# One matmul stage by a rank-20 block algorithm in place of 22 block products, with new sums of its inputs

## The chip, the cores and the metric

One core of one Trainium2 chip runs the whole program in one launch. The metric is the device time of the launch in microseconds (us); three runs of the kernel before took 589.03, 589.66 and 590.48 us (median 589.66).

## The reference

`r`, `k`, `v`, `w` have batch 4, 8 heads, 768 steps and 48 features a head; everything is float32.

```
state = 0
for t in range(768):
    cur  = (u*k[t]) outer v[t]
    y[t] = r[t] @ (state + cur)
    state = w[t][:, None]*state + k[t] outer v[t]
x   = y as 3072 tokens x 384 features
h   = x @ w_in            # 384 x 2048
g   = 0.5*h*(1 + erf(h/sqrt(2)))
out = g @ w_out           # 2048 x 384
```

The change concerns `h = x @ w_in` and, through its results, the sums of `g` that feed the last product.

## The kernel before, in words

The 3072 tokens are eight tiles of 384 tokens (`T`). For tile x there is `attention(x)`, which leaves the tile's y transposed in `xT` (3 blocks of 128 features by 384 tokens), and `mlp(x)`, which makes h, GELU and the output. Both are Python generators that yield after each small piece. While `mlp(x-1)` runs, the main loop also runs most of `attention(x)` and the first steps of `attention(x+1)`: a string `PLAN[x]` has one letter for each piece to be issued next ("." is `mlp`, "s" the attention slots of this tile, "f" the following tile's, "x" the sums of xT, "w" masks and sums of weights, "l" loads, "c" conversion of weights). There is no scheduler: each engine works off its own queue in exactly the order in which the letters issue. The queues are TensorE (PE), VectorE (DVE), ScalarE (ACT), GpSimd (POOL, here only the issuing of DMAs that add to memory) and SyncE (SP, loads and stores).

**h in mlp(1) to mlp(7)** (`h_halves`, matmuls at L929). The tokens are cut in halves of 192, the features in three blocks of 128, and w_in's columns in two halves; 22 block products replace 24 by means of sums of blocks. It goes in four rounds (q), each for two blocks of 128 columns from each half. One `two(...)` with one pair of factors is two matmuls of 128x128 by 128x192. Seven sub-steps a round leave their results in three PSUM banks; ACT copies a bank to another bank (L972) or to g (L995, L999) or to a buffer `o_sb` (L965), and a finished block goes through GELU (L961, L958). What is saved in `o_sb` is added to g by a DMA that accumulates, issued by POOL (L980), in the first three rounds, and by DVE (L982) in the last. The sums of xT are five DVE instructions (`sums_of_x`, L897); the sums of w_in are made once by DVE (`h_sums`, L880 to L888), between mlp(0) and mlp(1).

**The output** is a second set of block products (L1073) over g, over sums of g (`of_g`, L921 to L925, DVE) and over sums of w_out. Its first product reads blocks of g for the first 128 tokens, its second those of the second 128 tokens, its third needs an ACT copy of the first (`p1`, L1109).

**Attention beside it.** In tiles 2 to 7 (`quarters`) DVE multiplies and reduces r, k and w (L378, L385, L411, L419), ACT and DVE lay out `kx` (L557, L562, L563), PE then makes scores into a pair of banks `d` (L588, L579), which DVE and ACT copy out (L621, L604). DVE updates r and k (L642, L649, L653), and after a second round of the same PE makes kv and y (L711, L752, L797). At the end of a tile ACT copies y to xT (L820, L823), SP moves 16 rows of it (L827), and DVE makes the sums of xT for the next mlp.

PSUM holds two banks `mm` (h and o), two banks `u` and two pairs `d`. A bank can be written again only when its last reader is done. mlp(0) makes h without sums (L1059).

Of the kernel before, what the change touches and what calls it, by code (L numbers as in the profile page):

```python
# [10 lines left out]
F32 = mybir.dt.float32  # L11
# [31 lines left out]
        "ccclfccccccfccfcccccfccfccwf.ff......fw.sl.w.x.wx...x..x...xww"  # L43
    ),
    2: (
        "s.s.....ss....ssw.ws.wl.wsss.wws.s..lsl...lws.w..s.ww....s.s..l..sss.lssss....s..s..s.sls."
        "llsf.sf.fs..fl.xx.x.fxx"
    ),
    3: (
        "ls.ls....lss..ss.....ss..l.s.lsss.sss.s.s.s.ss..sss..sssssss....s.s..l...s..l.sslslsf.ffs."  # L50
        "..x.lx..xxx"
    ),
    4: (
        "lls.s.sss..s.l.........ssss.....sss.s.ss.s..s.sllss...s.s..l.sss.ss..s.ss...s..sslsll.s..f"
        ".sf.sf..ff..xx.xflxx"
    ),
    5: (
        "..ss...s..ssl....sls...s.sss..sss..sss.sls...sllss..sssss.s..l..s.s...s.slll..s.ssfsf.fsf."
        "....xxx.lxx"
    ),  # L60
    6: (
        "ss..sss...s.....s.sl..s...l.s.ssls.s.s..s..sssssl......ss.ssss.sl.sl...s.....ss..llsssl.f."
        "s.fsf.f.f.xx.l.xffxx"
    ),
    7: "....ss.s...s.s.s....s.sss..ss.ss.sss..s..sss..sssssss......s.s....s..ssss.s...x.x..xxx",
}

# [6 lines left out]
def kernel(  # L74
# [276 lines left out]
    xT_of = {}  # L351

    def attention(x, unit):
# [14 lines left out]
        if x not in xT_of:  # L368
            xT_of[x] = wk.tile([128, NJ, T], F32, name="xT")
        xT = xT_of[x]  # L370
# [483 lines left out]
    HK = HF // 2  # L854
    s_of, x_sums, s12_of = [], [], {}

    def homes():

        more = [cv.tile([128, PIECE], I64, name="s", tag="raw", bufs=AHEAD).bitcast(F32) for _ in range(2)]
        s3_sb.append(more[0][:, 0:HF * 128].rearrange("p (f c) -> p f c", f=HF))  # L860
        x_sums.extend(z[:, i * HT:(i + 1) * HT] for z in (more[0][:, HF * 128:], more[1][:, HF * 128:]) for i in range(2))
        spare = [cv.tile([128, PIECE], F32, name=name) for name in ("f", "f", "e", "e")]
        for i, name in enumerate(("s1", "s2")):
            s12_of[name] = [z[:, 0:FG * 128].rearrange("p (f c) -> p f c", f=FG) for z in spare[2 * i:2 * i + 2]]
        second = [more[1][:, i * WI:(i + 1) * WI] for i in range(HK)]
        third = [s_home[:, i * WI:(i + 1) * WI] for i in range(HK)]
        fourth = [z[:, FG * 128:] for z in spare]
        s_of.extend((second, third, fourth))

    def h_sums():  # L870

        def w(a, c, k):
            return w_in_sb[:, a * HK + k * 2:a * HK + k * 2 + 2, c, :]

        def pieces_of(i, k):
            return s_of[i - 2][2 * k:2 * k + 2]

        for k in range(2):
            for i in range(2):
                nc.vector.tensor_sub(pieces_of(3, k)[i], w(0, 0, k)[:, i], w(1, 0, k)[:, i])  # L880
            yield
            nc.vector.tensor_add(w(1, 0, k), w(1, 0, k), w(1, 1, k))
            yield
            for i in range(2):
                nc.vector.tensor_sub(pieces_of(2, k)[i], w(1, 0, k)[:, i], w(0, 0, k)[:, i])
            yield
            for i in range(2):
                nc.vector.tensor_sub(pieces_of(4, k)[i], w(0, 1, k)[:, i], pieces_of(2, k)[i])  # L888
            yield

    def sums_of_x(x):

        xT = xT_of[x]
        x00, x01, x10, x11, l0, l1 = (xT[:, c, b * HT:(b + 1) * HT] for c in range(3) for b in range(2))
        t2, t3, t4, l01 = x_sums
        for o, a, b in ((t3, x11, x01), (x01, x01, x00), (t2, x11, x01), (t4, x10, t2), (l01, l0, l1)):
            nc.vector.tensor_sub(o, a, b)  # L897
            yield

    def mlp(x):  # L900
# [3 lines left out]
        xT = xT_of.pop(x)  # L904
# [26 lines left out]
        late = []  # L931

        def h_halves():

            x00, t1, x10, x11, l0, l1 = (xT[:, c, b * HT:(b + 1) * HT] for c in range(3) for b in range(2))
            t2, t3, t4, l01 = x_sums

            def w(a, c):
                return lambda f: w_in_sb[:, (a * HF + f) // FI, c, f % FI * 128:(f % FI + 1) * 128]

            def s(i):
                return w(1, 0) if i == 1 else lambda f: s_of[i - 2][f // FI][:, f % FI * 128:(f % FI + 1) * 128]

            def two(o, q, *factors, start=False):
                for i in range(2):
                    for n, (lhs, rhs) in enumerate(factors):
                        multiply(o[:, i * HT:(i + 1) * HT], lhs(2 * q + i), rhs, start and i == n == 0)

            def of_two(o):
                return o.rearrange("p (f t) -> p f t", f=2)  # L950

            def g_of(q, a, b):
                return gs[2 * a + 2 * q // FG][:, 2 * q % FG:2 * q % FG + 2, b * HT:(b + 1) * HT]

            def gelu(q, a, b, z):
                o = g_of(q, a, b)
                if waits and b:
                    nc.scalar.activation(out=o[:, :, 0:256 - HT], in_=z[:, :, 0:256 - HT], func=AF.Gelu)  # L958
                    f = a * HF + 2 * q
                    o, z = alone[:, f:f + 2], z[:, :, 256 - HT:]  # L960
                nc.scalar.activation(out=o, in_=z, func=AF.Gelu)  # L961

            def saved(o):
                z = wk.tile([128, DM], F32, name="o_sb", bufs=2)
                nc.scalar.copy(out=z, in_=o)  # L965
                return of_two(z)

            def first(q):
                a_of[q] = h_bank()
                two(a_of[q], q, (w(0, 0), x00), start=True)  # L970
                u_of[q] = bank_u(q)[:, 0:2 * HT]
                nc.scalar.copy(out=u_of[q], in_=a_of[q])  # L972

            def second(q):
                two(a_of[q], q, (w(0, 1), x10), (w(0, 2), l0))
                gelu(q, 0, 0, of_two(a_of[q]))

            def add_to(q, z, g):
                if q < HK - 1:
                    nc.gpsimd.dma_start(out=g, in_=z, accum_op=ALU.add)  # L980
                else:
                    nc.vector.tensor_add(g, g, z)  # L982

            def third(q):
                two(z_of[q], q, (s(4), x11), (w(0, 2), l1))
                add_to(q, saved(z_of[q]), g_of(q, 0, 1))

            def fourth(q):
                two(u_of[q], q, (w(1, 1), t4), (w(1, 2), l01))
                gelu(q, 1, 0, of_two(u_of[q]))  # L990

            def fifth(q):
                z_of[q] = h_bank()
                two(z_of[q], q, (s(1), t1), start=True)
                nc.scalar.copy(out=g_of(q, 1, 1), in_=of_two(z_of[q]))  # L995

            def sixth(q):
                two(u_of[q], q, (s(2), t2))
                nc.scalar.copy(out=g_of(q, 0, 1), in_=of_two(u_of[q]))  # L999

            def seventh(q):
                two(u_of[q], q, (s(3), t3), (w(1, 2), l1))
                add_to(q, saved(u_of[q]), g_of(q, 1, 1))

            def h_bank():
                return bank("h_ps")[:, 0:2 * HT]

            a_of, z_of, u_of = {}, {}, {}
            for group in (0, 2, 1, 3):
                gs[group] = gp.tile([128, FG, T], F32, name="g")  # L1010
            for q in range(HK):
                first(q)
                yield
                if q:
                    third(q - 1)
                    if q > 1:
                        gelu(q - 2, 1, 1, g_of(q - 2, 1, 1))
                    yield
                    seventh(q - 1)
                    yield  # L1020
                else:
                    fifth(q)
                    yield
                second(q)
                yield
                if q:
                    fifth(q)
                    yield
                sixth(q)
                yield  # L1030
                if q:
                    fourth(q - 1)
                    gelu(q - 1, 0, 1, g_of(q - 1, 0, 1))
                    yield
            q = HK - 1
            seventh(q)
            gelu(q - 1, 1, 1, g_of(q - 1, 1, 1))
            yield
            third(q)
            for _ in of_g(0):  # L1040
                pass
            yield

            def rest():
                fourth(q)
                gelu(q, 0, 1, g_of(q, 0, 1))
                gelu(q, 1, 1, g_of(q, 1, 1))
# [270 lines left out]
```

## Time and profile before

| | |
|---|---|
| runs | 589.03, 589.66, 590.48 us |
| span of the profiled execution | 587.8 us (the page gives it no other time: the median run lies 1.9 us above) |
| granted TensorE clock, mean | 0.997 |
| DMAs that add to g (POOL) | 42 of 192 KB |
| MLP's first matmuls of h start at | 118.8, 190.8, 254.3, 325.7, 389.3, 460.6, 524.5 us |

Busy time by stretch, us:

| stretch | length | PE | DVE | ACT | POOL |
|---|---|---|---|---|---|
| 0 to 44 | 44.0 | 32.2 | 34.2 | 17.4 | 8.0 |
| 44 to 115, with mlp(0) | 71.0 | 71.0 | 61.6 | 57.5 | 0.0 |
| 115 to 187, mlp(1) | 72.0 | 72.0 | 58.4 | 33.8 | 7.3 |
| 187 to 254, mlp(2) | 67.0 | 66.3 | 50.3 | 32.5 | 7.2 |
| 254 to 322, mlp(3) | 68.0 | 68.0 | 55.4 | 33.0 | 7.2 |
| 322 to 389, mlp(4) | 67.0 | 66.7 | 51.2 | 32.7 | 7.2 |
| 389 to 460.6, mlp(5) | 71.6 | 71.1 | 57.7 | 33.5 | 7.2 |
| 460.6 to 524.5, mlp(6) | 63.9 | 63.6 | 41.0 | 32.4 | 7.2 |
| 524.5 to 555, mlp(7), h | 30.5 | 30.5 | 3.9 | 15.5 | 7.2 |
| 555 to 588, mlp(7), output | 33.0 | 29.8 | 11.7 | 3.2 | 0.0 |

In a timeline each row is: start, length (both us from the span's start), engine, line, operation, output and input, shape, count, and in brackets how long the engine had been idle and what ended that. One matmul in the program is two MATMUL records in the trace (float32 goes in two passes). Rows of the chain of waits are start, length, engine, output, line and number of pieces.

### The profile page before, as it was taken

To read this page: it belongs to the slowest core of one execution; us is meant where nothing else is said; L and a number is where in the kernel's file an instruction comes from. 1 tells how busy PE (TensorE), PEld (TensorE's weight loads), DVE (VectorE), ACT (ScalarE), POOL (GpSimd) and SP (SyncE) were. 2 spreads that over 40 slices of the span, in tenths; PEclk is the share of its full clock that TensorE was granted. 3 is DMA by queue.
4 is the path that set the end of the run, shared out by engine and by line. 5 is a ranking of instruction groups with operands and counts; after the bars stand their busy time and mean duration, and the time that the engine had idled before them with its cause. 6 is when DMAs were issued, how large, how long until landed. Compare 5 with 4: busy or idle time off the path is not lost. (4 is left out here: it accounts for less than half of the span.)

```text
span 587.8 us, 17656 instructions
## 1 busy us (share of the span) xinstructions
PE 571.1 (97%) x7602; PEld 521.4 (89%) x7616; DVE 425.5 (72%) x825; ACT 291.2 (50%) x668; POOL 58.6 (10%) x63
## 2 busy tenths in 40 slices
PE   5789999999999999999999999999999999999997
PEld 3576666799999999999999999999998999999997
DVE  5988968989758975777959986777759987420332
ACT  2368898446362567235462467245561467335400
POOL 3100000013000130012000130002100111003100
PEclk8999999999999999999999999999999999999999
DMA  6749742253032542354122632344224333114201
GB/s 230 221 135 352 265 168 78 79 142 52 5 89 64 157 58 41 90 142 93 26 55 79 151 70 44 86 139 74 27 41 119 86 42 42 29 45 55 28 13 35
DMA packets 62430, 55.09 MB, mean 94 GB/s; under 512 B 32400, under 2 KB 47504, under 8 KB 62352
## 3 DMA queue, kind: packets, MB, share of 16 engines
q1 hardware_dynamic: 50832, 45.62, 25.5%
q0 software_dynamic: 11424, 8.26, 10.8%
q8 instruction: 60, 0.98, 0.7%
q14 instruction: 18, 0.15, 0.1%
q10 hardware_dynamic: 96, 0.07, 0.1%
HBM read 36.24 MB, written 4.72 MB: 70 GB/s over the span
## 5 line engine op out<-in xcount | busy, mean ns | idle before, releaser
L929 PE MATMUL h_ps<-xT,w_in_sb 128*128 128x192 f32 x560 | 111.5, 330 | 0.6 <-DVE o_sb L1196 0.6
L980 POOL DMA_DIRECT2D g<-o_sb x42 | 50.6, 1229 | 478.2 <-ACT o_sb L965 468.9
L929 PEld LDWEIGHTS h_ps<-xT,w_in_sb 128*128 128x128 f32 x560 | 93.0, 190 | 4.7 <-ACT g L961 1.6
L929 PE MATMUL u_ps<-s,w_in_sb 128*128 128x192 f32 x224 | 41.2, 327 | 0.0
L1073 PE MATMUL o_ps<-w_out_sb,g 128*128 128x192 f32 x224 | 39.8, 326 | 0.0
L929 PEld LDWEIGHTS u_ps<-s,w_in_sb 128*128 128x128 f32 x224 | 37.1, 190 | 0.2
L1073 PEld LDWEIGHTS o_ps<-w_out_sb,g 128*128 128x128 f32 x224 | 37.0, 190 | 0.0
L604 ACT COPY a_sb<-d 32x256 f32<-32x256 f32 (+8 forms) x90 | 32.6, 362 | 4.9 <-PE d L588 3.4
L1059 PE MATMUL h_ps<-xT,w_in_sb 128*128 128x384 f32 x96 | 33.2, 494 | 0.0
L452 PEld LDWEIGHTS d<-rkw 64*64 64x64 f32 x1152 | 19.4, 138 | 14.7 <-issue 10.5
L1073 PE MATMUL o_ps<-w_out_sb,f 128*128 128x192 f32 x176 | 32.0, 331 | 0.0
L1073 PE MATMUL o_ps<-t,g 128*128 128x192 f32 x176 | 31.4, 330 | 0.0
L1073 PE MATMUL o_ps<-t,s 128*128 128x192 f32 x176 | 31.2, 328 | 0.0
L1073 PE MATMUL o_ps<-t,e 128*128 128x192 f32 x176 | 30.6, 326 | 0.5 <-issue 0.5
L621 DVE COPY_PREDICATED a_sb<-quarter,d 128x480 f32<-128x480 uint8 (+5 forms) x54 | 23.2, 439 | 10.5 <-PE d L588 9.3
L726 DVE SCALAR_TENSOR_TENSOR st<-st,tot_sb,kv_ps 128x48 f32<-128x48 f32 x160 | 28.9, 258 | 2.6 <-PE kv_ps L711 2.5
L1073 PE MATMUL o_ps<-w_out_sb,e 128*128 128x192 f32 x176 | 30.7, 328 | 0.0
L982 DVE TENSOR_TENSOR g<-g,o_sb 128x384 f32<-128x384 f32 x14 | 7.6, 549 | 31.2 <-ACT o_sb L965 31.1
L1073 PEld LDWEIGHTS o_ps<-t,e 128*128 128x128 f32 x176 | 28.9, 190 | 0.7 <-issue 0.7
L1073 PEld LDWEIGHTS o_ps<-t,g 128*128 128x128 f32 x176 | 28.6, 190 | 0.5
L1073 PEld LDWEIGHTS o_ps<-w_out_sb,f 128*128 128x128 f32 x176 | 28.5, 190 | 0.6
L1073 PEld LDWEIGHTS o_ps<-t,s 128*128 128x128 f32 x176 | 28.8, 190 | 0.2
(163 smaller groups left out, 1171.3 us busy)
## 6 DMA issues: line engine op xcount, KB each, us to landing
rkw<-in_rkw_dram SPq DMA_DIRECT2D x54, 256.0 KB, 3.6
g<-o_sb POOLq DMA_DIRECT2D x42, 192.0 KB, 3.6
raw<-in_w_out_dram SPq DMA_DIRECT2D x8, 768.0 KB, 6.2
v_in<-in_v_dram SPq DMA_DIRECT2D x8, 584.0 KB, 4.6
raw<-in_w_in_dram SPq DMA_DIRECT2D x5, 768.0 KB, 7.5
out_dram<-o_sb SPq DMA_DIRECT2D x20, 192.0 KB, 2.0
rkw<-kx SPq DMA_DIRECT2D x72, 48.0 KB, 2.0
rkw<-in_rkw_dram SPq DMA_DIRECT2D x6, 384.0 KB, 6.2
```

The lines of the kernel that those rows point to most:

```text
L452: nc.tensor.matmul(d[half[p], g, n * width:(n + 1) * width], lhsT=kc[half[g], b, i, p], rhs=right(half[g], b, i, p), start=True, stop=True)
L604: nc.scalar.copy(out=at[z, g, first:behind, (a + 1) * h:], in_=d[z, :, :, to] if g == slice(None) else d[z, :, to])
L621: nc.vector.copy_predicated(out=an[:, :, :, :, (a + 1) * h:], mask=mask.to_broadcast(data.shape), data=data)
L726: nc.vector.scalar_tensor_tensor(out=stq[:, q, c], in0=stq[:, q, c - 1] if c else b4[:, q, NC - 1], scalar=totq[:, q, c:c + 1], in1=kvs[q ...
L929: nc.tensor.matmul(o, lhsT=lhsT, rhs=rhs, start=start, stop=True, skip_group_check=True)
L980: nc.gpsimd.dma_start(out=g, in_=z, accum_op=ALU.add)
L982: nc.vector.tensor_add(g, g, z)
L1059: nc.tensor.matmul(h_ps, lhsT=w_in_sb[:, f // FI, j, f % FI * 128:(f % FI + 1) * 128], rhs=xT[:, j, :], start=(j == 0), stop=(j == NJ - 1))
L1073: nc.tensor.matmul(o, lhsT=lhs(j), rhs=rhs(j), start=start and j == 0, stop=(j == HF - 1), skip_group_check=True)
```

## The change

`h_halves` becomes `h_forms`. w_in's columns are now cut in four quarters (j), w_in's rows in three blocks (c) and the tokens in two halves (a), and the eight blocks of h come from 20 products (`PRODUCTS`: accumulator, block or sum of w_in, block or sum of xT, whether it starts a bank) in two rounds (q). Each product is two matmuls of 128x128 by 128x192, as before. `STEPS` writes out the order by hand. In a step, `P7` is product 7; `1a10` copies bank a to g's block (token half 1, quarter 0); `=cb` and `=db` copy bank b (for d, negated) to a bank `u`; `se`, `sd+1`, `sa`, `sb-` save a bank in `o_sb` (with `-`, negated); `me>00` adds what was saved to block 00 of g by an accumulating DMA; `+d10`, `-c02`, `-b13` are DVE instructions that add or subtract a bank to or from a block of g; `g00` is GELU in place (a digit more names the round) and `G01` GELU from bank a. `TAIL` is issued in the middle of the first output product. Five of the 19 sums of w_in are accumulating DMAs too (marked `d`). Sums of xT become eleven, in one buffer `forms_x` and in place; `xT` is one buffer. `o_sb` has six buffers, the scratch for descriptors of POOL's DMAs is set to 8192, and `PLAN[1]` to `PLAN[7]` have more letters.

In the order of the changed program's instructions, the three DVE instructions `+d10`, `-c02`, `-b13` of round 0 stand behind attention's L563 (L623 in the new numbering) in tiles 2, 4, 5 and 6, behind it and three more in tile 1, and ahead of it in tile 3.

```diff
+OUTS = 6
+FORMS_W = {
+    "minus e0": ("e0", "-", "w01", "w00"),
+    "e5h": ("e5", "+", "w20", "w22"),
+    "h02": ("w02", "+", "w00", "w02"),
+    "e1": ("e1", "+", "w12", "w02"),
+    "e2h": ("e2", "+", "w11", "e1"),
+    "w13h": ("w13", "d", "w13", "e2"),
+    "e3": ("e3", "-", "e1", "w01"),
+    "w11": ("w11", "-", "w10", "w11"),
+    "e4": ("e4", "-", "w21", "w11"),
+    "e2": ("e2", "d", "e2", "w21"),
+    "e7": ("e7", "-", "e4", "e5"),
+    "e6": ("e6", "+", "w03", "w13"),
+    "w21": ("w21", "d", "w21", "e6"),
+    "w01": ("w01", "d", "w01", "e6"),
+    "w23": ("w23", "d", "w23", "w21"),
+    "w13": ("w13", "-", "w13", "w02"),
+    "w03": ("w03", "-", "w23", "w03"),
+    "w02": ("w02", "-", "w03", "w02"),
+    "e5": ("e5", "+", "w02", "e5"),
+}
+FORMS_X = (
+    ("f0", "+", "x01", "x11"),
...
+    ("f9", "n", "f5", "x12"),
+)
+PRODUCTS = {
+    0: ("a", "w10", "x01", True), 7: ("a", "e4", "f4", False), 4: ("a", "w11", "f2", False),
+    9: ("a", "e6", "f7", False), 10: ("a", "w21", "f6", False), 19: ("a", "w01", "x00", False),
+    17: ("b", "e2", "f0", True), 5: ("b", "e1", "f1", False), 8: ("b", "w12", "x11", False),
+    2: ("b", "w02", "f5", False), 11: ("b", "w13", "f8", False), 18: ("b", "w23", "f9", False),
+    3: ("e", "w00", "x00", True), 12: ("e", "w20", "x02", False),
+    1: ("c", "w03", "f3", False), 6: ("c", "e5", "x02", False),
...
+STEPS = (
+    (
+        "P3", "P12 se", "P17 =cb", "P0 1a00 me>00", "P5 =db", "P1 1c03", "P7 1a10", "P8 1b12", "P15 sd+1", "P4 1a11 md1>11",
+        "P6", "P2 1b02 me>02", "P13", "P16 sd+2 md2>12", "P9 1a13 g00", "P11 sb- mb>03", "P10 sa ma>03", "P14 +d10 -c02",
+        "P18 -b13", "P19 G01 g11",
+    ),
+    (
+        "P3 g020", "P12 se g100", "P17 =cb", "P0 1a00 me>00 g130", "P5 =db g120", "P1 1c03 g030", "P7 1a10", "P8 1b12", "P15 sd+1", "P4 1a11 md1>11",
...
+        "P18 -b13", "P19 G01 g02 g12",
+    ),
+)
+TAIL = "g13 g03 g10 g11"
...
-    xT_of = {}
+    xT = const.tile([128, NJ, T], F32, name="xT")
...
-    def h_sums():
...
+    def h_sums(names):
+
+        for name in names:
+            o, sign, *ab = FORMS_W[name]
+            o, a, b = (w_block(z) for z in (o, *ab))
+            op = nc.vector.tensor_add if sign == "+" else nc.vector.tensor_sub
+            if sign == "d":
+                nc.gpsimd.dma_start(out=o, in_=b, accum_op=ALU.add)
...
     def sums_of_x(x):
 
-        xT = xT_of[x]
-        x00, x01, x10, x11, l0, l1 = (xT[:, c, b * HT:(b + 1) * HT] for c in range(3) for b in range(2))
-        t2, t3, t4, l01 = x_sums
-        for o, a, b in ((t3, x11, x01), (x01, x01, x00), (t2, x11, x01), (t4, x10, t2), (l01, l0, l1)):
-            nc.vector.tensor_sub(o, a, b)
+        for o, sign, a, b in FORMS_X:
...
-        def h_halves():
...
+        def h_forms():
...
+            def run(q, what):
+                kind, arg = what[0], what[1:]
+                if kind == "P":
+                    z, w, xf, fresh = PRODUCTS[int(arg)]
+                    if fresh:
+                        banks[z] = bank("h_ps") if z in "ab" else bank_u(0)
+                    o = banks[z][:, 0:HK * HT]
+                    for i in range(HK):
+                        multiply(o[:, i * HT:(i + 1) * HT], of_q(w_block(w), q)[:, i * 128:(i + 1) * 128], x_form(xf),
+                                 fresh and i == 0)
+                elif kind == "=":
+                    z, y = arg[0], arg[1]
+                    o = bank_u({"c": 1, "d": 0}[z])
+                    copy(o[:, 0:HK * HT], banks[y][:, 0:HK * HT], z == "d")
+                    banks[z] = o
+                elif kind == "1":
+                    copy(g_of(q, arg[1:]), of_two(banks[arg[0]][:, 0:HK * HT]))
+                elif kind == "s":
+                    z = wk.tile([128, DM], F32, name="o_sb", bufs=OUTS)
+                    copy(z, banks[arg[0]][:, 0:HK * HT], arg[1:2] == "-")
+                    saved[arg[0] + arg[2:]] = of_two(z)
+                elif kind == "m":
+                    t, h = arg.split(">")
+                    nc.gpsimd.dma_start(out=g_of(q, h), in_=saved[t], accum_op=ALU.add)
+                elif kind in "+-":
+                    o = g_of(q, arg[1:])
+                    (nc.vector.tensor_add if kind == "+" else nc.vector.tensor_sub)(o, o, of_two(banks[arg[0]][:, 0:HK * HT]))
...
-            yield from h_halves()
+            yield from h_forms()
...
             for _ in product(o1, of_blocks(0, 0), of_w(0, 0), True):
                 yield
-                for z in late:
-                    z()
+                if fast:
+                    for what in TAIL.split():
+                        tail(what)
...
-        yield from h_sums()
+        yield from h_sums(FORMS_W)
...
-    nc = _bacc.Bacc("TRN2", target_bir_lowering=False, num_devices=1)
+    nc = _bacc.Bacc("TRN2", target_bir_lowering=False, num_devices=1, dynamic_dma_scratch_size=8192)
```

## The prediction on record

> **What bounds the kernel now.** I read the page's busy row first.
>
> ```profile
> PE 571.1 (97%) x7602; PEld 521.4 (89%) x7616; DVE 425.5 (72%) x825; ACT 291.2 (50%) x668; POOL 58.6 (10%) x63
> L929 PE MATMUL h_ps<-xT,w_in_sb 128*128 128x192 f32 x560 | 111.5, 330 | 0.6 <-DVE o_sb L1196 0.6
> L980 POOL DMA_DIRECT2D g<-o_sb x42 | 50.6, 1229 | 478.2 <-ACT o_sb L965 468.9
> g<-o_sb POOLq DMA_DIRECT2D x42, 192.0 KB, 3.6
> ```
>
> PE is busy 97% of the span. The stretches of the small table above say where the rest is: the start and the last output; between 44 and 555 us PE is idle for about 2 us. The end is set by how much PE has to do, and each microsecond that PE newly waits counts in full. The second line has the h matmuls that the change makes fewer, the last two the accumulating DMAs that it doubles: POOL spends 1.23 us on an issue, and the sum lies in memory 3.6 us later (median; 3.4 to 6.3).
>
> Then the chain of waits and the timeline, for the price of a matmul and for how far DVE is from holding PE up. Tile 2 and tile 5 stand for the even and odd tiles.
>
> ```profile
> 336.22 1.95 PE h_ps L929 x12
> ```
>
> ```profile
> 190.81 2.22 PE L929 MATMUL h_ps<-xT,w_in_sb 128*128 128x192 f32 x12 [0.36 <-DVE o_sb L1196]
> ...
> 205.94 1.06 PE L588 MATMUL d<-kx,rkw 64*64 64x96 f32 x40 [0.36 <-DVE kx L563]
> ```
>
> ```profile
> 204.84 0.96 DVE L563 TENSOR_TENSOR kx<-kx,tot_sb 128x768 f32<-128x768 f32 x1 [0.40 <-ACT kx L557]
> ```
>
> ```profile
> 389.25 2.93 PE L929 MATMUL h_ps<-xT,w_in_sb 128*128 128x192 f32 x16
> ...
> 405.96 1.06 PE L588 MATMUL d<-kx,rkw 64*64 64x96 f32 x40
> ```
>
> ```profile
> 404.15 0.96 DVE L563 TENSOR_TENSOR kx<-kx,tot_sb 128x768 f32<-128x768 f32 x1 [0.40 <-ACT kx L557]
> ```
>
> 12 records take 1.95 us, so a program matmul (two records) takes 0.325 us. DVE works almost without a gap from a tile's sums of xT to L563, which ends 15.0 to 15.9 us after the tile's first h matmul (tile 2: 205.80 less 190.45, where PE would have begun without its wait; tile 5: 405.11 less 389.25). PE needs L563 for attention's scores and comes to them just then: 0.36 late in tile 2, on time in tile 5. DVE is no bottleneck by its 72%, but in this half of a tile it has no slack.
>
> **A. Fewer matmuls.** Before, 22 block products of 4 matmuls are 88 a tile; after, 2 rounds of 20 products of 2 are 80. 8 x 0.325 = 2.6 us a tile, seven tiles: **-18.2 us**. Everything on PE is on the path, so it counts whole.
>
> **B. The sums of w_in, first tile.** Eight DVE sums (12 instructions, about 5.8 us) become fourteen (9.7 us) and five DMAs. They are issued between mlp(0) and mlp(1), where DVE is full:
>
> ```profile
> 107.85 0.74 DVE L885 TENSOR_TENSOR s<-w_in_sb 128x256 f32<-128x256 f32 x2
> ...
> 114.91 0.72 DVE L888 TENSOR_TENSOR f<-w_in_sb,s 128x256 f32<-128x256 f32 x2
> ...
> 116.49 0.69 DVE L882 TENSOR_TENSOR w_in_sb<-w_in_sb 128x512 f32<-128x512 f32 x1
> ```
>
> From 107.85 on I laid out DVE's new order with these durations (0.69 long, 0.6 apart for a 128x512 sum, L419 and L385 as they stand): e2h is ready at 115.2. From there w13 += e2, e2 += w21, w21 += e6, w23 += w21 each wait for the one before. At 3.5 to 3.9 a hop, with the issue, e2 is whole at 123.2, and w23, then w03 by DVE, at 131.7. PE starts h at 118.8, reaches P17 (reads e2) two products of 0.65 later at 120.1 and waits 3.1; P1 (reads w03), three products on, waits 6.5. Together 9.6. DVE, which is held by w03, is then late for the scores (2.05) and for the second round's first product (1.0): **+12.6**, at least 9.6.
>
> **C. DVE between the rounds, tiles 2 to 6.** A round's 20 products take 13.0 us, with small waits for ACT 13.3. Its last banks (d, c, b) are now emptied by three DVE instructions, which stand in DVE's order behind L563 (ahead of it in tile 3), and the next round's first product P3 needs one of them. In front there are six sums of xT more, 0.33 apart: 2.0 us. Tile by tile, when DVE lets go and when PE asks:
>
> - tile 2: L563 ends 205.80, +2.0, +0.55 for `+d10` (a row like L982's, 549 ns) = 208.35; PE asks at 190.45+13.3 = 203.75. Wait 4.6.
> - tile 3: 271.6, +1.45 (0.55 falls into an idle gap), three adds 1.65 = 274.7; scores after 25 products at 270.95. Wait 3.7.
> - tile 4: 339.45+2.0 = 341.45; scores are ahead of the last product, 325.7+12.65 = 338.35. Wait 3.1.
> - tile 5: 405.1+0.95 (1.05 into a gap)+0.55 = 406.6; 389.25+13.3 = 402.55. Wait 4.05.
> - tile 6: 474.47+2.0 = 476.45; 460.63+12.65 = 473.3. Wait 3.15.
>
> Sum 18.6; the 0.36 and about 0.4 that PE waits there in tiles 2 and 4 now go: **+17.9**. PE's saved time is the reason: A brings PE to this point earlier, and DVE cannot follow, as its work starts with the xT that PE's own last tile gives. If the sums of xT were free, 2.0 would go in most tiles: lower bound 9. If attention's DVE rows also move later with PE's waits it is 18 or more.
>
> **D. The second round and the end.** In tile 2 I followed the rest. ACT has 44 operations a tile for 36, 0.48 each, and in this stretch two sets of attention's copies stand in its queue:
>
> ```profile
> 218.25 2.60 ACT L604 COPY a_sb<-d 32x320 f32<-32x320 f32 x6 [0.54 <-PE d L588]
> ...
> 222.13 2.58 ACT L604 COPY a_sb<-d 32x320 f32<-32x320 f32 x6
> ```
>
> A bank saved behind these is late for PE: 0.25+0.6+0.5+0.9 for single copies, 2.05 for `sb-` behind both sets. Then the tail: `G01` before the output's bank 0.75; block 03, which is sum on sum (`sb-`, DMA 3.6, DMA 3.6, GELU), 1.5 beyond the output products that do not read it; `p1`, queued on ACT behind three GELUs of the tail, 1.05. Together 7.6. Even tiles have this order: three times 22.8. In odd tiles attention's copies stand elsewhere: 1.5 each for three. The last tile has no attention, but no cover either: 2.3. All of it would be 29.6. I followed only one tile, and the other queues catch up while PE waits for one, so I take half: **+14.8**, bounds 3 and 29.6.
>
> **E. At no cost.** The issues of 47 more DMAs are POOL's, which is 10% busy. A negated copy: the nearest rows are 478 and 605 ns, I take 478, where it is already in the sums above. One `xT` in place of two: sums in place are on DVE's own queue, PE has read it long before; the next tile's y arrives after the h stage; 0, at worst a wait like the 1.03 of tile 2, seven times 7. The smaller descriptor scratch has no row; issues stand 1.25 us apart in pairs now and two transfers are under way at once. If one had to wait for the other it would be 3.6 less 1.25 = 2.3 for each pair, on the path only at the tail; I take 0, and the range holds 2.3 for some tiles. A gain there has no reason.
>
> **Sum.** -18.2 + 12.6 + 17.9 + 14.8 = +27.1. The profiled execution has a span of 587.8 and the median run is 1.9 more; both shift alike, so 589.7 + 27.1 = **617 us**.
>
> [...]
>
> **Rivals.**
>
> 1. *DVE is not late; faster.* Only the chain of w_in's sums (9.6) and the last tile's end (2.3) cost: 589.7-18.2+9.6+2.3 = 583. For it: DVE is 28% idle. Against: the rows above, no gap of a microsecond between xT and L563. It decides by whether L563 ends within 13.3 us of the tile's first product: it took 15.0 to 15.9. Chance 0.11, with the whole strip below 588.
> 2. *Half the waits.* B at 9.6, C at 9 to 13, D at 3: 593 to 597; with C and D milder still it goes down to 588, where the saving is just given back. Chance 0.17, a part of it near no change.
> 3. *All terms full*: 589.7-18.2+12.6+17.9+29.6 = 631.6, and with it more wherever a late DVE delays the next tile's attention too. For it: attention's order was only scaled. Chance 0.12 above 630.
> 4. *DVE holds up POOL's DMAs.* With 89 DMAs instead of 42, and each `mb`, `ma` pair in series, an issue that DVE delays by a microsecond would cost 14 on seven pairs of two: 631. Against it: the 42 issues have a median of 1.20 us and none is over 1.56, while DVE is busy 72%. Chance 0.05. [...]
>
> That the change does not do what it says is settled: fewer matmuls stand in the program. The forecast itself, 600 to 630, has 0.55.
>
> **Chances and range.** A measurement of this kernel tells about 0.3% (1.8 us) from no change. Faster by more: 0.11 (rival 1); within: 0.04 (the low end of rival 2); slower: 0.85 (forecast, rivals 3 and 4, the rest of 2). The range is 594 (B and D at their low ends, C at 9 to 10) to 634 (all terms full, and 2.3 for the scratch).
>
> **What would show it.** Right: 112 MATMUL records fewer in h, PE busy near 553 us at a share of about 90%; in the first tile PE idle at P17 after a DMA and at P1 after DVE's w03, ten us in all; in each of tiles 2 to 6 an idle stretch of 3 to 4.6 us before the second round's P3 or the first scores, put down to DVE's g or kx; idle before the output's matmuls after ACT and DMAs; POOL with 89 issues of still 1.2 us. Wrong: PE idle stays under 20 us in all, or L563's successor ends within 13 us of the tile's first product; landings well under 3.4 us or over 6.3 us; or the waits cost less because attention's DVE work shifts earlier with the shorter h stage.

## The result and the profile after

The changed kernel took 673.27 us (median of 6 runs, 670.53 to 678.96), the kernel before 590.07 beside it: a ratio of 1.143, with a 95% interval of 1.138 to 1.148. It is 83 us slower; 27 had been forecast, and the range ended at 634. The profiled execution has a span of 677.2 us, 89.4 more than before's; it is the slowest of the six (678.96 us), so the parts below add up to some 6 us more than the medians differ by.

The page of the changed kernel, its busy row, the row of the granted clock (tenths, 40 slices) and the rows of the accumulating DMAs:

```profile
PE 596.9 (88%) x7504; PEld 527.4 (78%) x7504; DVE 456.1 (67%) x897; ACT 312.7 (46%) x724; POOL 115.5 (17%) x110
...
PEclk9989999789979899997998989997998979899989
...
L1051 POOL DMA_DIRECT2D g<-o_sb x84 | 101.9, 1258 | 408.1 <-ACT g L1026 244.7
...
g<-o_sb POOLq DMA_DIRECT2D x84, 192.0 KB, 3.7
```

PE's share fell from 97% to 88%, as far as forecast. But its busy time did not fall to 553 us, it rose to 597, though h has 1120 MATMUL records in place of 1232. The clock row says why: before, every slice from the second on stood at 9; now it is 7 or 8 in a dozen of them. The DMAs are as quick as before: 1.26 us an issue (1.23 before), 3.7 us to the landing (3.6), at twice the number.

PE's waits, longest total first (us in all, times, longest):

```profile
PE o_ps L1100 <- ACT g L1064: 11.3, 9, 2.8
PE h_ps L1002 <- ACT o_sb L1024: 10.5, 4, 4.5
PE kv_ps L771 <- DMA rkw<-kx: 9.0, 4, 3.0
PE u_ps L1002 <- DVE w_in_sb L955: 7.8, 1, 7.8
PE h_ps L1002 <- ACT g L1026: 7.2, 3, 5.1
PE h_ps L1002 <- ACT g L1064: 4.4, 1, 4.4
PE h_ps L1002 <- DMA s<-w_in_sb: 4.0, 1, 4.0
PE u_ps L1002 <- DVE g L1054: 3.7, 1, 3.7
```

The rows with `w_in` are the first tile, the other h rows mostly the turn between the rounds in tiles 2 to 6, the first row the output's GELU, the third a wait in attention that no step of the prediction names. The last row is tile 5's turn.

What a long wait does to the clock is seen in tile 2, in stretches of 3.41 us (length, busy us of PE, PEld, DVE, ACT and POOL, then the granted clock):

```profile
225.70:229.11 3.41, 1.46 (x8) 1.17 (x8) 3.41 (x6) 0.39 (x1) 0.69 (x1) 1.00 0.89 118
229.11:232.52 3.41, 0.89 (x5) 0.89 (x6) 2.98 (x5) 2.09 (x5) 0.64 (x1) 1.00 0.51 154
232.52:235.94 3.42, 3.42 (x33) 2.98 (x35) 0.69 (x2) 1.40 (x4) 0.62 (x2) 0.50 0.44 58
235.94:239.35 3.41, 3.41 (x117) 2.79 (x110) 2.75 (x4) 0.99 (x3) 1.13 (x1) 1.00 0.49 62
```

PE waits 4.47 us until 231.6. The stretch in which it was busy 0.89 of 3.41 us is followed by one at half clock, although the wait is over and PE works through it. Every change of the clock in this trace falls on the same grid of 3.41 us, within 2 ns.

So the 89.4 us come apart (from 44 us on; in the first 44 us both traces have the same work, 1090 and 1089 weight loads):

| part | us | how |
|---|---|---|
| 56 matmuls fewer | -18.2 | 56 x 0.325 |
| PE idle | +66.8 | 71.8 for 5.0 |
| half clock | +26.1 | 20 stretches at 0.5, the last cut by the end; PE busy in them 52.3 us, half of it taken as lost |
| short waits inside PE's busy time | +14.6 | busy 561.4 - 26.1, less before's 538.9 - 18.2 |

The idle time by place, from the brackets of PE's timeline: first tile 13.2, between the rounds of tiles 2 to 6 21.5, kv in the odd tiles 9.6, the rest of the second round and of the output 22.6 (all beyond before's few).

### The profile page after: what moved, and what is told of

It reads as the page before. It is cut to its first block, busy times and chain, and to the rows that moved or that the text cites. A ratio compares the mean times of both kernels' runs of the same rounds, so it can differ in the third digit from the quotient of the medians.

```text
span 677.2 us, 17755 instructions
## 1 busy us (share of the span) xinstructions
PE 596.9 (88%) x7504; PEld 527.4 (78%) x7504; DVE 456.1 (67%) x897; ACT 312.7 (46%) x724; POOL 115.5 (17%) x110
## 3 DMA queue, kind: packets, MB, share of 16 engines
q1 hardware_dynamic: 50832, 45.62, 22.6%
## 4 chain that ended last, share of the span: by engine, by line
PE 39%; DVE 16%; issue 15%; DMA 13%; ACT 9%; POOL 4%; SPq 3%; ACTq 0%; POOLq 0%; DVEq 0%
PE o_ps L1100 16%; DMA g<-o_sb 8%; PE h_ps L1086 5%; POOL g L1051 4%; DVE rkw L479 4%; PE h_ps L1002 4%; PE d L512 4%; PE u_ps L1002 2%; DVE kx L445 2%; PE kv_ps L771 2%; PE d L648 2%; DVE rkw L438 2%; ACT a_sb L664 2%; ACT g L1064 2%; PE y_ps L812 2%
## 5 line engine op out<-in xcount | busy, mean ns | idle before, releaser
L1051 POOL DMA_DIRECT2D g<-o_sb x84 | 101.9, 1258 | 408.1 <-ACT g L1026 244.7
L1002 PE MATMUL h_ps<-forms_x,w_in_sb 128*128 128x192 f32 x280 | 60.1, 343 | 18.1 <-ACT o_sb L1024 10.5
L1002 PEld LDWEIGHTS h_ps<-forms_x,w_in_sb 128*128 128x128 f32 x280 | 47.4, 195 | 23.8 <-ACT o_sb L1024 11.7
L1064 ACT ACTIVATE g<-g 128x384 f32<-128x384 f32 x74 | 36.9, 520 | 39.1 <-DMA g<-o_sb 36.8
L1026 ACT COPY g<-h_ps 128x384 f32<-128x384 f32 x84 | 39.7, 481 | 20.2 <-PE h_ps L1002 18.4
L1100 PEld LDWEIGHTS o_ps<-w_out_sb,g 128*128 128x128 f32 x224 | 38.6, 200 | 9.6 <-DVE g L1054 4.0
L1002 PE MATMUL h_ps<-forms_x,s 128*128 128x192 f32 x168 | 37.7, 349 | 5.1 <-DMA s<-w_in_sb 4.0
L1100 PEld LDWEIGHTS o_ps<-t,g 128*128 128x128 f32 x176 | 31.9, 209 | 12.0 <-ACT g L1064 11.3
L1002 PE MATMUL h_ps<-xT,w_in_sb 128*128 128x192 f32 x168 | 37.1, 346 | 4.4 <-ACT g L1064 4.4
L1002 PE MATMUL u_ps<-xT,w_in_sb 128*128 128x192 f32 x168 | 35.2, 346 | 3.7 <-DVE g L1054 3.7
L681 DVE COPY_PREDICATED a_sb<-quarter,d 128x480 f32<-128x480 uint8 (+5 forms) x54 | 23.2, 438 | 17.9 <-PE d L648 16.7
L1054 DVE TENSOR_TENSOR g<-g,u_ps 128x384 f32<-128x384 f32 x28 | 14.4, 546 | 29.9 <-PE u_ps L1002 28.5
L1002 PEld LDWEIGHTS h_ps<-xT,w_in_sb 128*128 128x128 f32 x168 | 29.6, 199 | 6.1 <-ACT g L1064 4.7
L1002 PEld LDWEIGHTS u_ps<-xT,w_in_sb 128*128 128x128 f32 x168 | 29.5, 200 | 5.0 <-DVE g L1054 4.0
```

The costliest lines, as they stand in the source:

```text
L681: nc.vector.copy_predicated(out=an[:, :, :, :, (a + 1) * h:], mask=mask.to_broadcast(data.shape), data=data)
L1002: nc.tensor.matmul(o, lhsT=lhsT, rhs=rhs, start=start, stop=True, skip_group_check=True)
L1026: nc.scalar.copy(out=o, in_=z)
L1051: nc.gpsimd.dma_start(out=g_of(q, h), in_=saved[t], accum_op=ALU.add)
L1054: (nc.vector.tensor_add if kind == "+" else nc.vector.tensor_sub)(o, o, of_two(banks[arg[0]][:, 0:HK * HT]))
L1064: nc.scalar.activation(out=o, in_=z, func=AF.Gelu, scale=s)
```

## The experiments

The columns of this table are worked out from each trace as above (one execution each, so they need not match the medians to the microsecond); "short" is PE's busy time after 44 us, less the clock's part, less 520.7.

| kernel | median, us | ratio to before, 95% | PE idle | half clock | short |
|---|---|---|---|---|---|
| changed kernel | 673.3 | 1.143 (1.138 to 1.148) | 71.8 | 26.1 | 14.6 |
| e1, one wait in before | 594.8 | 1.010 (1.007 to 1.012) | 8.2 | 1.7 | - |
| e2, four waits filled | 667.7 | 1.133 (1.128 to 1.137) | 56.0 | 19.6 | - |
| e3, w sums by DVE | 666.3 | 1.131 (1.127 to 1.136) | 64.9 | 24.4 | 14.4 |
| e4, scratch in before | 588.6 | 0.999 (0.997 to 1.001) | - | - | - |
| e5, pieces moved | 611.4 | 1.040 (1.037 to 1.042) | 29.9 | 4.4 | 9.7 |
| e6, e5 and e3 | 600.7 | 1.020 (1.017 to 1.022) | 23.4 | 0 | 10.5 |
| e7, block 03 | 642.4 | 1.090 (1.086 to 1.094) | 49.6 | 15.2 | 10.0 |
| e8, five sums of xT | 664.6 | 1.129 (1.125 to 1.133) | 62.0 | 23.7 | 14.6 |
| e9, moved in h alone | 634.7 | 1.079 (1.073 to 1.085) | 44.1 | 12.4 | 10.9 |
| e10, e3, e7 and e9 | 611.7 | 1.038 (1.036 to 1.040) | 30.8 | 2.5 | 10.3 |
| e11, e3, e7, all moved | 594.5 | 1.008 (1.005 to 1.011) | 17.1 | 1.7 | 6.7 |
| e12, as e11, moved again | 597.7 | 1.015 (1.012 to 1.018) | 21.3 | 1.7 | 8.4 |

Theory: the order of the queues makes PE wait in three places (the sums of w_in, the turn between the rounds, the output behind block 03), and each long wait is followed by a granted clock of 0.50, as in the stretches above. Rivals: a wait costs its length alone; DVE and ACT are too full for any order; the DMAs are the limit.

**e1, one wait in the kernel before**

```diff
+            for _ in range(16 if x == NX - 1 and o is t2 else 1):
                 nc.vector.tensor_sub(o, a, b)
```

> The kernel before with one sum of xT made 16 times ahead of the last tile's h (the same result each time), so that PE has one wait of about 4.2 us there and everything else stays. Theory (a long wait halves TensorE's clock for the next 3.4 to 6.8 us): the time rises by the wait and 1.7 to 3.4 us more, by 6 to 7.6 us, and the clock's rows show 0.5 behind the wait. Rival (a wait costs its own length alone): 4.2 us and a clock of 1.0 throughout.

Measured: 1.0097, which is 5.7 us (4.4 to 7.1). The row of PE's timeline behind the sums, and two stretches around it:

```profile
530.27 0.92 PE L930 MATMUL u_ps<-s 128*128 128x192 f32 x4 [3.89 <-DVE s L898]
...
533.07 0.85 PE L930 MATMUL h_ps<-xT,f 128*128 128x192 f32 x2
```

```profile
528.13:531.54 3.41, 1.27 (x8) 1.27 (x9) 2.54 (x8) 0.26 (x1) 0.00 (x0) 1.00 0.00 0
531.54:534.95 3.41, 3.41 (x12) 3.41 (x11) 0.00 (x0) 1.03 (x3) 0.00 (x0) 0.50 0.00 0
```

The wait is 3.89 us; in the stretch after it two records take 0.85 us where 0.49 is usual, and the clock is 0.50. 3.9 and, for half of that stretch, 1.7 make 5.6. The agreement to 0.1 is partly chance: by the table the trace has 8.2 less 5.0, 3.2 us, more of idle time, as small waits elsewhere are shorter, and 4.9 with the clock's 1.7. Both sums lie in the interval of 4.4 to 7.1, and neither 3.9 nor 3.2 alone does: the clock's theory holds, the rival falls. The expected 6 to 7.6 was a little high, since the wait is shorter than 4.2 and a single stretch followed it.

**e2, four waits filled with work**

```diff
+FILL = {(2, "P14"): 14, (4, "P14"): 12, (5, "P14"): 12, (6, "P16"): 17}
...
+    if q == 0 and FILL.get((x, what)):
+        for _ in range(FILL[x, what]):
+            multiply(banks["d"][:, HK * HT:], w_block("w00")[:, 0, 0:128], x_form("x00")[:, 0:128])
     run(q, what)
```

> The changed kernel with 12 to 17 matmuls more per tile in tiles 2, 4, 5 and 6, written to 128 unused columns of the bank that the waiting product does not need, just ahead of the long wait between the rounds: PE works 2.6 to 3.7 us of the 3.3 to 5.1 us that it would have waited, and nothing becomes ready earlier. Theory (clock): in these four places the clock stays at 1.0, which gives back what six half-speed windows of 3.4 us took, 9 to 12 us, though PE has 55 matmuls more to do. Rival (the waits alone count): no change against the changed kernel, within 2 us, or slower by the matmuls where they do not fit.

Measured: 5.6 us less than the changed kernel, and the two intervals do not meet, with 55 matmuls more. PE behind the filling in tile 2, and the stretch that follows:

```profile
228.29 0.92 PE L1003 MATMUL h_ps<-forms_x,w_in_sb 128*128 128x192 f32 x4 [1.40 <-ACT o_sb L1025]
```

```profile
225.65:229.07 3.42, 2.02 (x15) 1.73 (x14) 2.99 (x5) 2.09 (x5) 0.53 (x1) 1.00 0.49 153
229.07:232.48 3.41, 3.41 (x61) 2.84 (x64) 1.68 (x4) 1.51 (x5) 0.67 (x1) 1.00 0.47 62
```

In all four places the clock stayed at 1.00 (in tiles 2, 4 and 6 the 4 records next behind the filling took 0.82 us; usual are 0.81 to 0.92). The gain is less than the 9 to 12 expected: the lost clock fell by 6.5 us only. The six stretches went, but a wait for kv in tile 5 now lowered the clock for two stretches and not for one (16 records of the output behind it took 4.61 us, in the changed kernel 3.17), and a wait of 2.66 us in tile 2's output lowered it (4 records in 1.65 us behind it) where one of 2.45 had not (0.92). By the grid of each trace the wait of 2.66 us, 257.14 to 259.80, falls almost whole into one stretch, 256.37 to 259.78; the one of 2.45, 262.08 to 264.53, is cut by a line of the grid at 263.24. That part of the expectation was too high; that work without use makes the kernel faster, no price by length allows.

**e3, the sums of w_in by DVE**

```diff
-    "w13h": ("w13", "d", "w13", "e2"),
+    "w13h": ("w13", "+", "w13", "e2"),
...
```
(so for all five)

> The changed kernel with the five accumulating DMAs of the sums of w_in made by DVE in the same order. Theory (the chain of DMAs holds PE 12 us in the first tile, and the clock with it): the waits at P17 and P1 shrink from 11.9 to about 5 us, and the time falls by 7 us and by some 3 us of clock, 10 us in all. Rival (DVE is the bound there, and five sums of 0.6 us more make it later by 3): 3 us or less.

Measured: 7.0 us less. The first tile went from 94.8 to 88.3 us; the waits there are now 1.58 for a sum of xT, 2.95 for DVE and 1.93 for ACT, 6.5 in place of 13.2. So the chain of DMAs is worth half of the first tile's 13.2 us; the other half is still there when DVE does the sums, 4.5 of it in waits for DVE, which is late itself. Between the two expectations, nearer to the first. In the mended order (e5 to e6) the same edit takes away 10.7 us.

**e4, the smaller scratch in the kernel before**

```diff
-    nc = _bacc.Bacc("TRN2", target_bir_lowering=False, num_devices=1)
+    nc = _bacc.Bacc("TRN2", target_bir_lowering=False, num_devices=1, dynamic_dma_scratch_size=8192)
```

> The kernel before with the smaller scratch for descriptors of POOL's DMAs alone. Theory (it costs nothing; pairs of DMAs still run at once): same time within 1 us, landing still 3.6 us. Rival (it holds the second of a pair back): landing of some over 5 us, up to 2.3 us on the path.

Measured: no difference (0.997 to 1.001), landing 3.4 to 6.1 us with a median of 3.6, as before. The scratch is out.

**e5 and e6, attention's pieces moved**

PLAN[1] to PLAN[7] keep their letters in sequence; only the dots between them move. As an example, the first row of PLAN[6], the pieces of attention(6) beside mlp(5)'s h:

```diff
-        "ss..sss...s........s..sl..s.....l.s..sslss..s....s..sssssl..........ss.ssss.sl.sl...s....."
+        ".......s.....s.sss..ss..s.l..s..l..s.s.slss.ssss......ss...s.l..ss..sssss...l.sls....ss.ll"
```

> The changed kernel with the same work in another order: the letters of PLAN[1] to PLAN[7] keep their sequence, but the mlp's steps between them are set anew, so that PE, ACT and DVE come to each other's results later (in tiles 2 to 6 mostly by moving attention's pieces some steps behind the end of the first round). Nothing is added or left out. Theory (it is the order of the queues that makes PE wait, and the waits that lower the clock): the waits between the rounds and the waits for attention's moves of k fall to about 1 us each, the clock stays at 1.0 outside the first tile, and the time falls by 60 to 75 us, to 595 to 612. Rival (DVE and ACT have too much to do beside the shorter h, or the 84 accumulating DMAs are too slow): the waits move elsewhere, and the time stays over 640.

> The same with the five accumulating DMAs of w_in's sums made by DVE as well. Theory: the first tile's wait of 12 us goes to some 3 us, 7 to 10 us less than with the slots moved alone: 587 to 602, with PE's waits under 25 us in all and no half clock behind them. Rival (the terms are one wait, and what is taken away here comes back there): no better than the slots alone.

Measured: 611.4 and 600.7 us. The first is 62 us less than the changed kernel with the same instructions; PE's idle time fell from 71.8 to 29.9 and the clock's part from 26.1 to 4.4, all of it between 117 and 141 us, about the first tile's start, and with the sums by DVE to nothing. The clock's row of e5's page:

```profile
PEclk9999999888999999999999999999999999999999
```

What the order does is seen on ACT, at the turn between the rounds of tile 2. The changed kernel:

```profile
225.57 0.52 ACT L1064 ACTIVATE g<-g 128x384 f32<-128x384 f32 x1
229.86 1.34 ACT L617 COPY kx<-rkw 128x384 f32<-128x384 f32 x3 [3.77 <-DVE rkw L479]
231.10 0.48 ACT L1024 ACTIVATE o_sb<-h_ps 128x384 f32<-128x384 f32 x1
```

and e6:

```profile
205.70 0.47 ACT L1024 ACTIVATE o_sb<-h_ps 128x384 f32<-128x384 f32 x1
206.25 0.48 ACT L1026 COPY o_sb<-h_ps 128x384 f32<-128x384 f32 x1
...
211.69 1.33 ACT L617 COPY kx<-rkw 128x384 f32<-128x384 f32 x3
```

ACT has next to nothing to do at 226 us. But attention's copy L617 stands ahead of the save L1024 (`sb-`) in its queue, waits 3.77 us for DVE, and PE, which needs the bank that `sb-` frees, waits 4.47. In e6 the save stands ahead, and L617 waits for nobody. The rival, that DVE and ACT have too much to do, falls: DVE is busy 456.1 and 457.0 us, ACT 312.7 and 314.1. Nor are the accumulating DMAs the limit: e5 has all 89 of them.

**e7, block 03 in the second round**

```diff
-        ... "P11 sb- mb>03", "P10 sa ma>03", ...
+        ... "P11 sb-", "P10 sa vb>03 ma>03", ...
...
+                elif kind == "v":
+                    t, h = arg.split(">")
+                    nc.vector.tensor_add(g_of(q, h), g_of(q, h), saved[t])
```

> The changed kernel with one edit in the second round: of the two accumulating DMAs in series that block 03 of g needs, the first (mb>03) becomes a DVE addition out of the same buffer, put just ahead of the second, so the last GELU waits for one landing and not for two. Theory (the late GELU of block 03 holds DVE's sums of g, these hold attention's last update of k and its twelve moves on SP, and these hold PE at kv): PE's waits at kv in the odd tiles (9 us in all) and most of those of the output (11 us, for GELU) go, and the clock windows behind them, so the time falls by 18 to 30 us from 673. Rival (the landings are hidden behind the output's products, and kv is late since DVE is busy): 5 us or less.

Measured: 31 us less than the changed kernel (642.4), just over the 18 to 30 expected, for one landing in place of two in each tile. The waits for kv's moves of k went from 9.0 us to under 1, those of the output for GELU from 11.3 to 3.1, and the clock lost 15.2 instead of 26.1. How a GELU reaches kv, in tile 1 of the changed kernel (a DVE, an SP and a PE row):

```profile
175.47 0.69 DVE L994 TENSOR_TENSOR f<-g 128x512 f32<-128x512 f32 x1 [7.11 <-ACT g L1064]
```

```profile
184.69 9.04 SPq L591 DMA_DIRECT2D rkw<-kx  x12
```

```profile
194.52 0.31 PE L771 MATMUL kv_ps<-v_in,rkw 64*64 64x48 f32 x2 [2.66 <-DMA rkw<-kx]
```

DVE stands 7.11 us before the sums of g, for the GELU of block 03 that waits for two landings. Behind these sums are attention's updates of k and its transposes; SP issues the twelve moves of k only then, 0.75 us each, and PE's kv comes 2.66 us too early. In e7 the same DVE row waits 2.45 us, and SP begins 60 us after the tile's first product, not 64.6.

**e8, five of eleven sums of xT**

```diff
+            if x > 1 and name in ("f3", "f4", "f5", "f6", "f7", "f8"):
+                pass
```

> The changed kernel with six of the eleven sums of xT left out from the second tile on, so that h is computed from sums of an earlier tile; all else is as it was. Theory (between the rounds PE waits for DVE, which is later by these sums): the five waits there shrink by 1 to 2 us each, 8 us in all, and the clock windows behind some of them go: 8 to 20 us less than 673. Rival (the sums fall into gaps of DVE): no change within 3 us.

Measured: 8.7 us less. The waits between the rounds shrank (for `sb-` from 10.5 to 6.7, for the copies of tile 6 from 5.1 to 3.0), the clock's part by 2.4. DVE's six sums are a real but small part of being late.

**e9, moved beside h alone**

PLAN[3] to PLAN[7] have e5's places in the 40 steps of h, and the old, scaled ones behind.

> The changed kernel with the moved order of attention's pieces only where they stand beside the 40 steps of h in tiles 2 to 6; beside the first tile and the output products the order is the old one, scaled. Theory (the waits between the rounds and their clock windows are some 21 and 14 us): 30 to 40 us less than 673, the rest of the 62 us lying in the output's part and in tile 1. Rival (order between the rounds is a small part): less than 15 us.

Measured: 38.6 us less, as expected. Between the rounds of tiles 2 to 6 only waits of up to 1.7 us are left, and kv still waits 8.4 us:

```profile
PE kv_ps L771 <- DMA rkw<-kx: 8.4, 4, 3.0
PE u_ps L1002 <- DVE w_in_sb L955: 7.8, 1, 7.8
PE o_ps L1100 <- ACT g L1064: 4.3, 6, 1.3
```

**e10, three single edits together**

> The changed kernel with the three single edits of earlier runs together: the sums of w_in by DVE (7 us less alone), block 03's first addition by DVE in the second round (31 less), and attention's pieces moved in the h steps of tiles 2 to 6 (38.6 less). Theory (three separate causes, each with its own clock windows): they add up, 673 less 76.6, so 592 to 602. Rival (they share the same lost time): over 612.

Measured: 611.7, 61.6 us less, where the sum was 76.6: nearer to the rival's 612 than to the expected 592 to 602. They share 15 us. In tile 6 e7 alone saves 5.0 us, e9 alone 13.5, both 12.8: moved pieces of attention already free the GELU's way there. "Three separate causes" was too simple; the odd tiles add up better (tile 3: 7.5 and 8.4 alone, 12.3 together).

**e11 and e12, everything moved**

Their PLAN rows are again only other places for the same letters; both have the edits of e3 and e7.

> The three edits, with attention's pieces moved in tile 1 and in the output's part too. Theory: no wait over 2.5 us and no half clock behind 44 us; what is left against the kernel before is 18.2 us of matmuls less and some 20 us of short waits more: 585 to 597. If it comes out under 588 the change pays once its order fits; rival (short waits on banks stay, since DVE and ACT have more to do in each round): 590 or more, not faster than before.

> As e11, with the pieces beside the first tile moved once more, since e11's first h started 3.6 us later than before (a wait of 2.4 us for ACT ahead of it, and a half clock behind that). Theory (that start is the larger part of the 5 us by which e11 is slower): the first h starts at 119 to 120 us, no half clock there, and 588 to 592 us, about the time of before: the 18.2 us of matmuls are spent on some 18 us of short waits. Rival (the wait moves to another place): 594 as e11.

Measured: 594.5 and 597.7 us, 0.8% (0.5 to 1.1) and 1.5% slower than before. e11's page:

```profile
PE 565.1 (96%) x7504; PEld 505.5 (86%) x7504; DVE 460.1 (78%) x909; ACT 313.6 (53%) x724; POOL 101.1 (17%) x98
```

Against before, e11's trace has 18.2 us of matmuls less, 12.1 us of idle more (17.1 for 5.0), 6.7 us of short waits and 1.7 of clock: +2.3, and its span is 2.5 longer (it is the fastest of its six runs; the medians are 4.9 apart). Its first h starts 3.6 us late, behind a wait for ACT of 2.4; e12 was to mend that, and moved it into mlp(0), where the first h starts at 125.0 (a wait for attention's kv, and a half clock at 84 us). Its expectation failed: the wait moved to another place, as the rival said, and the time is even 3 us above e11's. No kernel tried here beats the one before.

## Why the prediction was wrong

The side was right, and so was the place of every large wait but one (kv). The size was not: 89.4 us for 27.1. Of the 62.3 that were missing, the lowered clock is 26.1, D 17.4, the short waits 14.6, C 3.6 and B 0.6.

- **The step that failed** stands in the first paragraph: "each microsecond that PE newly waits counts in full". Here it counted for more. The whole sum prices a wait at its length; at each of the seven waits of 3.0 to 5.1 us after the first tile the granted clock then stood at 0.50 for 3.4 or 6.8 us. With the others, 20 stretches in all, that is 26.1 us that no term holds, and no rival held either, which is one reason why even "all terms full" ended at 631.6. Every stretch from 44 us on had a clock of 1.00 in the trace of before, with 5.0 us of idle time in all; but the first slice of the page's clock row, an 8, and the 0.96 of the first 44 us, where PE does wait, were there to be asked.
- **A**, -18.2: right. 56 matmuls are gone.
- **B**, 12.6: 13.2 measured, 4.0 at P17 (3.1), 7.8 at P1 (6.5), 1.3 behind. Single landings of the 256 KB took 3.8 to 3.9 us from the start of the issue, pairs 5.4 to 6.0. POOL's issue is 1.2 to 1.3 of that. From its end to the landing it is 2.6. So the estimate of 3.5 to 3.9 a hop, with the issue, holds for single DMAs of 256 KB.
- **C**, 17.9: 21.5 measured; by tiles 4.5, 5.0, 3.3, 3.7 and 5.1 for 4.6, 3.7, 3.1, 4.05 and 3.15. In tile 5 it is DVE's addition, as written. In tiles 2, 3, 4 and 6 the same late DVE reaches PE another way, over ACT: `sb-`, `G01` or a copy of a bank stands behind L617, and L617 waits for DVE's L479 (3.77, 5.99, 2.60 and 5.01 us). In tile 3 the three additions were done long before. ACT and PE there:

```profile
308.93 1.34 ACT L617 COPY kx<-rkw 128x384 f32<-128x384 f32 x3 [5.99 <-DVE rkw L479]
310.17 0.48 ACT L1064 ACTIVATE g<-h_ps 128x384 f32<-128x384 f32 x1
310.70 1.36 PE L1002 MATMUL h_ps<-xT,w_in_sb 128*128 128x192 f32 x4 [4.38 <-ACT g L1064]
```

The cause, DVE's lateness, was right: L563's successor L623 ended 15.6 to 20.0 us after the tile's first product. The path was wrong in four tiles of five, and the sum came near because both paths hang on the same DVE rows; that tiles 2 and 4 agree to 0.2 is luck. The starts of h before were also misread in tiles 2 and 4:

```profile
189.64 0.81 PE L929 MATMUL h_ps<-xT,w_in_sb 128*128 128x192 f32 x4
```

The first products stand at 189.64 and 325.00, not at 190.8 (190.45 without its wait) and 325.7. So L563 ended 13.8 to 17.3 us after them in tiles 2 to 6, where the prediction has 15.0 to 15.9; all are over its 13.3.

- **D**, 14.8: 32.2 measured, the second step that failed. I had worked out 29.6 and took half, since "the other queues catch up while PE waits for one". They do not: in order, what stands behind a late instruction is late too, and 9.6 us of it went by a path that I did not follow, GELU, DVE's sums of g, SP's moves, kv. e7 shows it: one landing less takes away most of both (kv from 9.0 to under 1, GELU from 11.3 to 3.1).
- **E**: right in its parts. The scratch costs nothing (e4, 0.999), the issues nothing (1.26 us each, 1.23 before). The short waits inside PE's busy time, 14.6 us, were in no term. Counted by what the matmuls write, at the granted clock, 6.4 of them lie in the products of h, 6.1 in the output's and 1.5 in kv; what ends them the traces do not show, and their cause stays open.
- Rival 4, that DVE holds up POOL's DMAs, is not seen: 84 issues at 1.26 us, landings of 3.4 to 5.7, with DVE busy 67%.
- Rival 1's condition, no wait on DVE, was nearly made by moving the pieces (in e11 the longest is 1.42 us), and even so the time is 594 and not 583: 12.1 us of idle time and 6.7 of short waits take what the matmuls give.

## What to carry to other kernels

In a kernel whose PE was 97% busy, each of the seven waits of 3.0 to 5.1 us that the edit opened after the first tile cost its length and then the work lost in one or two stretches of 3.41 us at a granted clock of 0.50, by this 1.7 to 3.4 us at the most; price both. In hand-ordered queues, look at what stands behind a waiting instruction on every engine that it feeds, also on one that is idle half the time, and follow a late result to the end before giving a discount. An order that fitted the old step lengths is not carried over by scaling: here it was worth 62 of 83 us.

## What the runs showed of the hardware

All of this is read from the profiles of this case. In the changed kernel's trace the granted clock of TensorE is 1.00 or 0.50, and every change of it lies on one grid of 3.41 us, within 2 ns. From 44 us on, each of the 12 stretches of the grid at 1.00 in which PE was busy for at most 1.34 us was followed by one at 0.50, and each of the 154 in which it was busy for 1.46 us or more by another at 1.00. Of the stretches at 0.50, the 11 in which PE was busy for 3.20 us or more were followed by one at 1.00, and the 8 in which it was busy for at most 3.18 by another at 0.50. The two stretches shown of e1 and e2 agree: 1.27 us busy, then 0.50; 2.02 us busy, then 1.00.

So waits of 2.24 and 2.80 us in the changed kernel's output lowered the clock, with PE busy 1.30 and 0.71 us of the stretch that held most of them, and one of 2.45 us did not: it lies in two stretches, in which PE was busy 2.25 and 1.83 us.
